# Attention sum, normaliser and output factor read from PSUM; the state's update as four column operations

## Chip, cores, metric

One core of a Trainium2 chip runs the whole program. The metric is the device time of one execution in microseconds (us). The engines are TensorE (PE, with its weight loads as PEld), VectorE (DVE), ScalarE (ACT), GpSimd (POOL) and SyncE (SP, which issues most transfers).

## The reference

Three layers follow each other: a gated linear attention (mLSTM), a mixture of experts with the best two of eight, and a gated feed-forward layer. The change is in the first. For 2 batches of 8 heads, 768 steps and head size 40 it computes:

```python
for t in range(S):
    m_new = np.maximum(f_gate[:, :, t] + m, i_gate[:, :, t])
    f_stab = np.exp(f_gate[:, :, t] + m - m_new)
    i_stab = np.exp(i_gate[:, :, t] - m_new)
    m = m_new
    C = f_stab[..., None, None] * C + i_stab[..., None, None] * np.einsum('bhd,bhe->bhde', vt, kt)
    n = f_stab[:, :, None] * n + i_stab[:, :, None] * kt
    h_tilde = np.einsum('bhde,bhe->bhd', C, qt)
    nq = np.einsum('bhd,bhd->bh', n, qt)[:, :, None]
    y[:, :, t] = 1.0 / (1.0 + np.exp(-o_gate[:, :, t])) * h_tilde / np.maximum(np.abs(nq), 1.0)
x = y.transpose(0, 2, 1, 3).reshape(B * S, H * D)
x = moe(x)          # top 2 of 8 experts, 320 -> 1024 -> 320
out = (silu(x @ w_gate) * (x @ w_val)) @ w_out   # 320 -> 1536 -> 320
```

## The kernel before

The 768 steps of a batch are cut into 6 chunks of 128 steps, so that there are 12 chunks `j`: 0 to 5 belong to the first batch, 6 to 11 to the second, and `c = j % 6` is the place within the batch. The recurrence is computed chunk by chunk. `scores` (L270) multiplies keys by queries, `weigh` (L278) multiplies the scores by decay weights that ACT and POOL have made (`prep_w`, L258), and `intra` (L307) multiplies the weights by the values, 41 columns a head (40 values and a column of ones, which gives the normaliser). Its result lies in columns 0 to 327 of a PSUM bank, `PY[j]`. `inter` (L290) multiplies the queries by the state of the earlier chunks, and `inter_y` (L299) scales that into an SBUF tile `t1`. `state` (L314) lets PE add this chunk's keys by values into columns 328 to 491 of the same bank, two heads above each other, so that four blocks `a` of 41 columns hold all eight; DVE multiplies the running state `Cs` by its decay (L328) and adds the bank's part (L329), and ACT copies `Cs` into `Cb` (L332), the operand of the next chunk's `inter`. In chunk 0 of a batch there is no earlier state, and `Cs` is copied (L326).

`norm` (L334) adds the two parts into an SBUF tile `y` (L338; a copy, L340, where c is 0), and makes the reciprocal of max(|n·q|, 1) in a small tile `dn` (L342 to L344). `x` holds the sigmoid of the output gate, and `emit_b` (L355) multiplies it by `y`, `emit_a` (L350) by `dn`. For chunk 0 `emit_a` runs on POOL. Then PE transposes `x` of that chunk (`gate_t`, L363, into a bank `pg`), and `gate_l` (L372) multiplies it by the router's weights.

The order on each engine is the order in which the code emits. Four strings of letters set it, one for the start and one each for the second, the middle and the last chunk; each letter calls one function with a chunk number. The one for the middle chunks is:

```python
BODY = 'GKzcWSdiwddctpqdyacdsdnmdvclcdde'
```

Here S is `scores` of the next chunk, i `inter`, w `weigh` of the next chunk, t `gate_t` of the chunk before, y `inter_y`, a `intra`, s `state`, n `norm`, m `emit_b`, l `gate_l` of the chunk before and e `emit_a`. So on PE the transposition of chunk j-1 (t) stands ahead of `intra` of chunk j (a), and waits for the last DVE operation of chunk j-1 (e). The letters d and c let in steps of the router (`route`, L376) and of its scatter by POOL; p lets in a piece of the experts' weights, which ACT rounds (L541) and POOL, in this stage, subtracts from the original (L542).

`PY[j]`, `pg` and a few others take turns in two PSUM banks of a pool named `po`. After the attention the experts (L641, L678) and the feed-forward layer (L641, L860) run on PE almost without a gap.

Of the kernel before, what the change touches and what calls it, by code (L numbers as in the profile page):

```python
# [7 lines left out]
F32 = mybir.dt.float32  # L8
# [5 lines left out]
OP = mybir.AluOpType  # L14
AX = mybir.AxisListType

B, H, S, D = 2, 8, 768, 40
# [11 lines left out]
DA = D + 1  # L29
# [59 lines left out]
def kernel(ctx, tc, qk, kvh, og, gates, cst, wgn, noise, w1, w2, w13, w2o, out):  # L89
    nc = tc.nc  # L90
    v, s, g, pe, sy = nc.vector, nc.scalar, nc.gpsimd, nc.tensor, nc.sync
# [52 lines left out]
    xs = dr.tile([NR + 2 * N, DM], F32, name="xs")  # L144
# [12 lines left out]
    at = atts.enter_context(tc.tile_pool(name="at", bufs=2, side="right", reuse_waits="tile"))  # L157
    eg = at.tile([128, NC, 2, 16], F32, name="eg", bufs=1)
    bc = at.tile([128, NC, 16], F32, name="bc", bufs=1)
    dec = at.tile([128, 8, NC], F32, name="dec", bufs=1)  # L160
    QK, KV, GB, W8, KS, YT, PY, PS = {}, {}, {}, {}, {}, {}, {}, {}
# [89 lines left out]
    Cs = at.tile([128, 4, DA], F32, name="Cs", bufs=1)  # L251
# [62 lines left out]
    def state(j):  # L314
        b, c = divmod(j, NC)
        if c == NC - 1:
            return
        va = KV[j][:, :, D:D + DA]
        q = H * DA
        for h in range(H):  # L320
            o = (h % 2) * 64
            pe.matmul(PY[j][o:o + 64, q + (h // 2) * DA:q + (h // 2 + 1) * DA], KS[j][:, h, :], va[:, h, :],
                      start=True, stop=True)
        pk = PY[j][:, q:q + 4 * DA].rearrange("p (a d) -> p a d", d=DA)
        if c == 0:
            v.tensor_copy(Cs, pk)  # L326
        else:
            v.tensor_tensor(out=Cs, in0=Cs, in1=dec[:, b * 4:b * 4 + 4, c, None].to_broadcast([128, 4, DA]), op=OP.mult)  # L328
            v.tensor_tensor(out=Cs, in0=Cs, in1=pk, op=OP.add)  # L329
        cb = Cb[(c + 1) % 2]  # L330
        for o in (0, 64):
            s.activation(cb[o:o + 64, :, o // 64, :], Cs[o:o + 64], AF.Copy)  # L332

    def norm(j):  # L334
        y = at.tile([128, H, DA], F32, name="y")
        py = PY[j][:, 0:H * DA].rearrange("p (h d) -> p h d", d=DA)
        if j % NC:
            v.tensor_tensor(out=y, in0=py, in1=YT[j], op=OP.add)  # L338
        else:
            v.tensor_copy(y, py)  # L340
        dn = at.tile([128, H], F32, name="dn")
        v.tensor_scalar(dn, y[:, :, D], -1.0, 1.0, op0=OP.mult, op1=OP.max)  # L342
        v.tensor_tensor(out=dn, in0=dn, in1=y[:, :, D], op=OP.max)
        v.reciprocal(dn, dn)  # L344
        YN[j] = (y, dn)

    def emit_a(j):
        y, dn = YN[j]
        xs = x[:, j, 0:DM].rearrange("p (h d) -> p h d", d=D)
        (v if j else g).tensor_tensor(out=xs, in0=xs, in1=dn[:, :, None].to_broadcast([128, H, D]), op=OP.mult)  # L350

    def emit_b(j):
        y, dn = YN[j]
# [653 lines left out]
    def early_piece(j):  # L1007
# [7 lines left out]
        "W": (2, prep_w),  # L1015
        "S": (1, scores), "K": (1, scale_k), "w": (1, weigh),
        "i": (0, inter), "y": (0, inter_y), "a": (0, intra), "s": (0, state),
        "n": (0, norm), "e": (0, emit_a), "m": (0, emit_b),
        "t": (-1, gate_t), "l": (-1, gate_l),
        "z": (0, lambda j: clear(3 if j == 2 else 2)), "p": (0, early_piece), "d": (0, lambda j: drip(1)), "c": (0, lambda j: drip_s(1)),  # L1020
# [149 lines left out]
```

## Time and profile before

| | us |
|---|---|
| median of 3 runs | 558.68 |
| the runs | 554.36, 558.68, 561.88 |
| the profiled execution | 555.08 |
| its span, first to last instruction | 553.4 |
| PE busy | 529.3 (96%) |
| DVE busy | 373.8 (68%) |
| ACT busy | 275.5 (50%) |
| POOL busy | 145.2 (26%) |

The attention takes about the first 116 us of the span. Busy shares are averages over all stages: PE is nearly always busy behind the attention and less so within it, so what DVE and POOL do matters in the attention first. PE matmul ends are modelled, and a few records can be missing. Starts are in us from the span's start, and an instruction of the same engine can begin a little ahead of the recorded end of the one in front of it.

### The profile page before, as it was taken

The page shows a single profiled execution, that of the slowest core. Times are in us where ns is not written, and L with a number is a line of the kernel's source. Part 1 is how long each engine was busy: PE and PEld are TensorE (multiplying, and loading weights), DVE is VectorE, ACT ScalarE, POOL GpSimd, SP SyncE. Part 2 cuts the span into 40 slices and gives each one's busy share as a digit, 9 for nine tenths or more (in the row PEclk, how much of TensorE's full clock was granted, in tenths as well). Part 3 has the DMA queues.
Part 4 walks back from the last instruction along what each step waited for, and adds up shares of the span by engine and source line. Part 5 has one row for each costly group of instructions (what it writes and reads, how often), then busy time and mean ns, then how long its engine had stood idle before and what let it go on. Part 6 is the DMA issues. An engine that isn't in the chain of part 4 may idle for free. (4 is left out here: it accounts for less than half of the span.)

```text
span 553.4 us, 9232 instructions
## 1 busy us (share of the span) xinstructions
PE 529.3 (96%) x3333; PEld 478.8 (87%) x3335; DVE 373.8 (68%) x833; ACT 275.5 (50%) x593; POOL 145.2 (26%) x175
## 2 busy tenths in 40 slices
PE   8998779889999999999999999999999999999997
PEld 4687678879898999989999999888888888888886
DVE  5584977858688897989898867787643434443332
ACT  5464545235566776876877664554332223222221
POOL 4153675455004432232322235233000000000000
PEclk8798877969999999999999999999999999999999
DMA  8799965553758787988987686461001000010001
GB/s 247 214 332 356 304 236 161 168 196 113 295 171 320 259 281 255 330 296 277 317 292 254 214 280 227 160 233 49 0 1 49 0 1 0 2 47 1 1 0 47
DMA packets 36882, 96.63 MB, mean 175 GB/s; under 512 B 4848, under 2 KB 17936, under 8 KB 36832
## 3 DMA queue, kind: packets, MB, share of 16 engines
q1 hardware_dynamic: 32208, 83.55, 44.9%
q0 software_dynamic: 2304, 7.87, 4.3%
q10 hardware_dynamic: 2320, 4.58, 2.4%
q8 instruction: 27, 0.44, 0.3%
q14 instruction: 23, 0.19, 0.1%
HBM read 72.70 MB, written 23.28 MB: 173 GB/s over the span
## 5 line engine op out<-in xcount | busy, mean ns | idle before, releaser
L678 PE MATMUL py<-wV,h 128*128 128x320 f32 (+1 forms) x624 | 106.6, 312 | 1.2 <-ACT ysb L689 0.8
L678 PEld LDWEIGHTS py<-wV,h 128*128 128x128 f32 (+1 forms) x624 | 95.6, 185 | 2.7 <-ACT ysb L689 1.2
L641 PE MATMUL ph<-xh,wU 128*128 128x416 f32 (+1 forms) x320 | 91.5, 336 | 0.4 <-PEq L719 0.4
L581 POOL TENSOR_TENSOR cq<-cq,csg 128x512 f32<-128x512 f32 (+1 forms) x27 | 38.5, 1425 | 121.0 <-ACT cq L580 96.7
L839 DVE TENSOR_TENSOR sg<-pg,sg 128x512 f32<-128x512 f32 x36 | 24.9, 691 | 58.2 <-ACT sg L838 58.2
L860 PE MATMUL py<-wV,uh 128*128 128x320 f32 x288 | 63.8, 309 | 0.0
L641 PEld LDWEIGHTS ph<-xh,wU 128*128 128x128 f32 x320 | 59.6, 195 | 2.5 <-ACTq L719 0.7
L542 DVE TENSOR_TENSOR wU<-stg,wU 128x512 fp32r<-128x512 f32 x72 | 54.1, 776 | 6.7 <-ACT wU L541 6.2
L838 ACT ACTIVATE sg<-pg 128x512 f32<-128x512 f32 x36 | 21.5, 598 | 66.0 <-PE pg L641 61.2
L848 ACT ACTIVATE uh<-u 128x512 fp32r<-128x512 f32 x36 | 22.8, 633 | 62.0 <-DVE u L840 62.0
L641 PE MATMUL ph<-xl,wU 128*128 128x416 f32 (+1 forms) x160 | 52.3, 327 | 0.1
L860 PEld LDWEIGHTS py<-wV,uh 128*128 128x128 f32 x288 | 49.5, 188 | 3.0
L641 PE MATMUL pg<-x2h,wU 128*128 128x512 f32 x144 | 51.4, 397 | 0.0
L641 PE MATMUL pv<-x2h,wU 128*128 128x512 f32 x144 | 50.6, 392 | 0.0
L541 ACT ACTIVATE wU<-stg 128x512 fp32r<-128x512 f32 x78 | 46.4, 624 | 7.4 <-DVE yt L687 4.6
L650 ACT ACTIVATE h<-ph 128x416 fp32r<-128x416 f32 (+1 forms) x80 | 35.6, 445 | 19.5 <-PE ph L641 17.6
L860 PE MATMUL py<-wV,ul 128*128 128x320 f32 x144 | 44.4, 309 | 0.0
L542 DVE TENSOR_TENSOR wV<-stg,wV 128x640 fp32r<-128x640 f32 x42 | 37.6, 906 | 3.4 <-ACT wV L541 3.3
L641 PE MATMUL ph<-xr,wU 128*128 128x416 f32 (+1 forms) x160 | 39.3, 327 | 0.3 <-DVE wU L542 0.3
L849 DVE TENSOR_TENSOR ul<-u,uh 128x512 fp32r<-128x512 f32 x36 | 24.9, 690 | 19.9 <-ACT uh L848 19.9
L777 POOL DMA_INDIRECT gy<-yg,ig__89 x24 | 25.2, 1051 | 48.0 <-DVE wU L542 26.8
L840 DVE TENSOR_TENSOR u<-pv,sg 128x512 f32<-128x512 f32 x36 | 24.9, 691 | 17.1 <-PE pv L641 16.7
(175 smaller groups left out, 1065.6 us busy)
## 6 DMA issues: line engine op xcount, KB each, us to landing
stg<-in_w_dram SPq DMA_DIRECT2D x20, 768.0 KB
stg<-in_w_dram SPq DMA_DIRECT2D x20, 640.0 KB
cw<-in_w_dram SPq DMA_DIRECT2D x18, 512.0 KB
gbt<-gp SPq DMA_DIRECT2D x10, 512.0 KB
f<-cq SPq DMA_DIRECT2D x18, 256.0 KB
stg<-f SPq DMA_DIRECT2D x6, 768.0 KB
kvt<-in_kvh_dram SPq DMA_DIRECT2D x12, 324.0 KB
QK<-in_qk_dram SPq DMA_DIRECT2D x24, 160.0 KB
```

Of the source, the lines that this page charges most:

```text
L541: s.activation(hi[:, c], ST[u][:, c], AF.Copy)
L542: (g if lo_pool[0] else v).tensor_tensor(out=lo[:, c], in0=ST[u][:, c], in1=hi[:, c], op=OP.subtract)
L581: g.tensor_tensor(out=q, in0=q, in1=sg, op=OP.mult)
L641: pe.matmul(ps_ap, a, b, start=(i == 0), stop=(i == len(seq) - 1))
L650: s.activation(h[:, 0:C], p[:, 0:C], AF.Relu)
L678: pe.matmul(yp[0:nr, 0:DM], x_, w, start=st and i == 0, stop=sp and i == 2)
L777: g.indirect_dma_start(out=y, out_offset=None, in_=yg[0:NR0] if j < NC else yg, in_offset=bass.IndirectOffsetOnAxis(ap=ig_[:, j, k:k + 1], ...
L839: v.tensor_tensor(out=sg, in0=pg, in1=sg, op=OP.mult)
L840: v.tensor_tensor(out=u, in0=pv, in1=sg, op=OP.mult)
L848: s.activation(uh, u, AF.Copy)
L849: v.tensor_tensor(out=ul, in0=u, in1=uh, op=OP.subtract)
L860: pe.matmul(OP_[q][a][:, 0:DM], x_[:, t], w[:, c], start=(f == 0 and i == 0), stop=(f == 11 and i == 2))
```

## The change

`norm` writes the sum back into the bank `PY[j]` in place of an SBUF tile, and leaves out the copy where c is 0: `y` is then the bank itself. A new small SBUF tile `dm` takes the first step of the normaliser; the second and the reciprocal are written into columns 492 to 499 of the same bank. `emit_b` and `emit_a` so read one operand from SBUF (`x`) and one from PSUM. `emit_a` of chunk 0 goes from POOL to DVE, as those of the other chunks. The state's decay and sum become one operation for each block of 41 columns, with the decay as one value a partition.

```diff
         else:
-            v.tensor_tensor(out=Cs, in0=Cs, in1=dec[:, b * 4:b * 4 + 4, c, None].to_broadcast([128, 4, DA]), op=OP.mult)
-            v.tensor_tensor(out=Cs, in0=Cs, in1=pk, op=OP.add)
+            for a in range(4):
+                v.scalar_tensor_tensor(Cs[:, a], Cs[:, a], dec[:, b * 4 + a, c:c + 1], pk[:, a], op0=OP.mult, op1=OP.add)
...
     def norm(j):
-        y = at.tile([128, H, DA], F32, name="y")
-        py = PY[j][:, 0:H * DA].rearrange("p (h d) -> p h d", d=DA)
+        y = PY[j][:, 0:H * DA].rearrange("p (h d) -> p h d", d=DA)
         if j % NC:
-            v.tensor_tensor(out=y, in0=py, in1=YT[j], op=OP.add)
-        else:
-            v.tensor_copy(y, py)
-        dn = at.tile([128, H], F32, name="dn")
-        v.tensor_scalar(dn, y[:, :, D], -1.0, 1.0, op0=OP.mult, op1=OP.max)
-        v.tensor_tensor(out=dn, in0=dn, in1=y[:, :, D], op=OP.max)
+            v.tensor_tensor(out=y, in0=y, in1=YT[j], op=OP.add)
+        dm = at.tile([128, H], F32, name="dm")
+        dn = PY[j][:, (H + 4) * DA:(H + 4) * DA + H]
+        v.tensor_scalar(dm, y[:, :, D], -1.0, 1.0, op0=OP.mult, op1=OP.max)
+        v.tensor_tensor(out=dn, in0=dm, in1=y[:, :, D], op=OP.max)
         v.reciprocal(dn, dn)
         YN[j] = (y, dn)
 
     def emit_a(j):
...
-        (v if j else g).tensor_tensor(out=xs, in0=xs, in1=dn[:, :, None].to_broadcast([128, H, D]), op=OP.mult)
+        v.tensor_tensor(out=xs, in0=xs, in1=dn[:, :, None].to_broadcast([128, H, D]), op=OP.mult)
```

On DVE, chunk 2 reads as follows before, from the scaling of the part of the earlier chunks to the weighing of the next scores (`t_526` is `t1`, `pg` the bank of the transposition, `W_487` the weights of chunk 4).

```order
L304 TENSOR_TENSOR t_526<-py,eg 128x328
L328 TENSOR_TENSOR Cs<-Cs,dec 128x164
L329 TENSOR_TENSOR Cs<-Cs,pY 128x164
L338 TENSOR_TENSOR y<-pY,t_526 128x328
L342 TENSOR_SCALAR dn<-y 128x8
L343 TENSOR_TENSOR dn<-dn,y 128x8
L344 RECIPROCAL dn<-dn 128x8
L355 TENSOR_TENSOR x<-x,y 128x320
L373 COPY lg<-pg 128x16
L350 TENSOR_TENSOR x<-x,dn 128x320
L281 TENSOR_TENSOR W_487<-pS,W_487 128x512 x2
```

The same chunk on DVE in the changed kernel, where the lines' numbers are those of the changed file:

```order
L304 TENSOR_TENSOR t_525<-py,eg 128x328
L329 SCALAR_TENSOR_TENSOR Cs<-Cs,dec,pY 128x41 x4
L337 TENSOR_TENSOR pY<-pY,t_525 128x328
L340 TENSOR_SCALAR dm<-pY 128x8
L341 TENSOR_TENSOR pY<-dm,pY 128x8
L342 RECIPROCAL pY<-pY 128x8
L353 TENSOR_TENSOR x<-x,pY 128x320
L371 COPY lg<-pg 128x16
L348 TENSOR_TENSOR x<-x,pY 128x320
L281 TENSOR_TENSOR W_486<-pS,W_486 128x512 x2
```

The decay no longer stands by itself ahead of the sum that needs PE's product; the rest keeps its place, with the bank in place of `y` and `dn`.

At the end of the start string, DVE before, from the first state (chunk 0) to the scaling in chunk 1:

```order
L326 COPY Cs<-pY 128x164
L340 COPY y<-pY 128x328
L342 TENSOR_SCALAR dn<-y 128x8
L343 TENSOR_TENSOR dn<-dn,y 128x8
L344 RECIPROCAL dn<-dn 128x8
L355 TENSOR_TENSOR x<-x,y 128x320
L1030 CAST slt<-ck 128x128
L281 TENSOR_TENSOR W_354<-pS,W_354 128x512 x2
```

And there now:

```order
L326 COPY Cs<-pY 128x164
L340 TENSOR_SCALAR dm<-pY 128x8
L341 TENSOR_TENSOR pY<-dm,pY 128x8
L342 RECIPROCAL pY<-pY 128x8
L353 TENSOR_TENSOR x<-x,pY 128x320
L348 TENSOR_TENSOR x<-x,pY 128x320
L1028 CAST slt<-ck 128x128
L281 TENSOR_TENSOR W_354<-pS,W_354 128x512 x2
```

The copy of 328 columns is gone, and `emit_a` of chunk 0 has come from POOL to stand behind `emit_b`. On PE, ACT and SP nothing changes its place.

## Rows read from the trace of the kernel before

**Rows 1.** Windows of 10 us: engines' busy us (instructions), PEclk, DMA share, GB/s.

```profile
40.00:50.00 10.00, 6.73 (x69) 5.75 (x67) 6.08 (x18) 4.27 (x14) 3.85 (x5) 1.00 1.04 373
...
80.00:90.00 10.00, 10.00 (x71) 9.14 (x71) 8.48 (x39) 4.14 (x12) 3.26 (x4) 0.55 0.57 189
```

**Rows 2.** The same view behind the attention (PE, PEld, DVE, ACT, POOL).

```profile
116.00:130.00 14.00, 13.91 (x80) 13.06 (x79) 7.15 (x43) 3.51 (x13) 5.90 (x11) 0.66 0.56 187
...
180.00:230.00 50.00, 50.00 (x303) 47.79 (x303) 43.88 (x86) 36.52 (x71) 17.29 (x15) 1.00 0.82 277
```

**Rows 3.** Waits of PE up to 116 us: total us, times, longest.

```profile
PE pg L363 <- DVE x L350: 9.4, 5, 4.5
```

**Rows 4.** Single lines: ns shortest/median/longest, first and last start.

```profile
L355 DVE TENSOR_TENSOR x<-x,y x12: 439/441/2096, 29.9 to 114.4; 128x320 f32<-128x320 f32 x12
...
L350 DVE TENSOR_TENSOR x<-x,dn x11: 478/492/841, 35.3 to 114.9; 128x320 f32<-128x320 f32 x11
...
L342 DVE TENSOR_SCALAR dn<-y x12: 170/171/1416, 28.9 to 112.2; 128x8 f32<-128x8 f32 x12
...
L338 DVE TENSOR_TENSOR y<-pY,t x10: 490/491/494, 33.8 to 111.6; 128x328 f32<-128x328 f32 x10
```

**Rows 5.** Timeline of DVE, chunks 6 and 7: start, us, operation [idle before].

```profile
74.84 0.33 DVE L326 COPY Cs<-pY 128x164 f32<-128x164 f32 x1 [3.79 <-PE pY L322]
75.09 0.49 DVE L340 COPY y<-pY 128x328 f32<-128x328 f32 x1
75.61 1.42 DVE L342 TENSOR_SCALAR dn<-y 128x8 f32<-128x8 f32 x1
77.06 1.22 DVE L343 TENSOR_TENSOR dn<-dn,y 128x8 f32<-128x8 f32 x1
...
78.91 0.80 DVE L350 TENSOR_TENSOR x<-x,dn 128x320 f32<-128x320 f32 x1
79.63 1.27 DVE L281 TENSOR_TENSOR W<-pS,W 128x512 f32<-128x512 f32 x2
80.83 0.17 DVE L397 TENSOR_TENSOR Lg<-ex,nz 128x24 f32<-128x24 f32 x1
81.03 0.18 DVE L398 TENSOR_TENSOR Lg<-Lg,lg 128x24 f32<-128x24 f32 x1
...
83.97 0.32 DVE L329 TENSOR_TENSOR Cs<-Cs,pY 128x164 f32<-128x164 f32 x1 [0.83 <-PE pY L322]
...
86.41 0.17 DVE L443 TENSOR_TENSOR pol<-pr,ck 128x24 f32<-128x24 f32 x1
```

**Rows 6.** Timeline of POOL around the same place and one chunk pair later.

```profile
78.50 0.87 POOL L267 TENSOR_SCALAR_AFFINE_SELECT W<-W 128x512 f32<-128x512 f32 x1 [0.25 <-ACT W L265]
...
101.15 1.29 POOL L542 TENSOR_TENSOR wU<-stg,wU 128x512 fp32r<-128x512 f32 x1
```

**Rows 7.** Timeline of PE, chunk 7.

```profile
79.86 0.52 PE L363 MATMUL pg<-ck,x 128*128 128x128 f32 x3 [2.07 <-DVE x L350]
```

**Rows 8.** Timeline of DVE, chunks 9 and 10.

```profile
99.40 0.32 DVE L329 TENSOR_TENSOR Cs<-Cs,pY 128x164 f32<-128x164 f32 x1 [1.18 <-PE pY L322]
99.64 0.49 DVE L338 TENSOR_TENSOR y<-pY,t 128x328 f32<-128x328 f32 x1
...
100.58 0.20 DVE L344 RECIPROCAL dn<-dn 128x8 f32<-128x8 f32 x1
100.70 2.10 DVE L355 TENSOR_TENSOR x<-x,y 128x320 f32<-128x320 f32 x1
...
106.82 0.32 DVE L328 TENSOR_TENSOR Cs<-Cs,dec 128x164 f32<-128x164 f32 x1
107.24 0.32 DVE L329 TENSOR_TENSOR Cs<-Cs,pY 128x164 f32<-128x164 f32 x1
107.48 0.18 DVE L417 TENSOR_TENSOR sel<-oh 128x24 f32<-128x24 f32 x1
```

**Rows 9.** Timeline of DVE in the experts: a small three-operand operation and its successor.

```profile
200.93 0.18 DVE L653 SCALAR_TENSOR_TENSOR h<-ph,h 128x32 fp32r<-128x32 f32 x1
201.03 0.58 DVE L627 TENSOR_TENSOR xl<-pxt,xh 128x416 fp32r<-128x416 f32 x1
```

## The prediction

> **What bounds the kernel now.** I read the busy time by stages first. Behind the attention PE has no gap: 50.00 of 50 us between 180 and 230 [rows 2]. So whatever moves the end of the attention, at about 116 us, moves the end of the program by as much. Within the attention no engine is full, and I ask which waits follow each other. The list of waits gives PE's largest one: 9.4 us in five waits, the transposition of a chunk waiting for `emit_a` of that chunk [rows 3]. PE is in order, so `intra` and `state` of the next chunk stand behind that wait; and DVE in turn waits for `state` before it can go on (0.83 and 1.18 us in two chunks) [rows 5, 8]. The path is a loop: DVE from the state's sum through norm and `emit_a`, PE from the transposition to `state`, DVE again.
>
> That holds from about 58 us on, chunks 4 to 11. Ahead of that the transfers are full (a share of 1.04 between 40 and 50 us, with PE busy for only 6.73 of 10) [rows 1]; what DVE saves or loses in chunks 0 to 3, the copy of chunk 0 and its `emit_a` from POOL among it, I count at nothing, with the key, query and gate loads as the cover. If that cover were gone, these chunks would pay or gain what the others do, a few tenths each.
>
> The last view is the one line by line. `emit_b` takes 441 ns in the median and once 2096; `emit_a` 492 and up to 841; the first step of the normaliser 171 and up to 1416 [rows 4]. All three work from SBUF alone. The sum, which has a PSUM operand, stays within 490 and 494 in all ten chunks [rows 4]. The stretched `emit_b`, at 100.70, runs beside a subtraction of weights on POOL from 101.15 that takes 1.29 us [rows 6, 8]. I read this as DVE and POOL keeping each other from SBUF, where the DVE operation needs nothing but SBUF operands. After the change none of these lines is such an operation.
>
> **The change part by part.** The terms are for the loop from 58 us on.
>
> 1. *Stalls of chunk 6.* The copy of 328 columns goes: its successor starts 0.52 us after it [rows 5]. The two first steps of the normaliser took 1.42 and 1.22 there against 0.17, so 1.25 and 1.05 us of stall go, and 0.31 of `emit_a`'s 0.80 against 0.49 [rows 4, 5]. That is 3.1 us on DVE. Not all of it is worth something. PE waited 2.07 us for this `emit_a` [rows 7], and that wait goes whole. But the next DVE work, the weighing, needs POOL's mask of the second half, which runs from 78.50 to 79.37 and depends on ACT, not on DVE [rows 6]. Its second half then takes some 0.6 us (half of 1.27 [rows 5]), so DVE reaches the router's first step at 80.0 and not at 80.83: 0.8 us. Further on it waited 0.83 us for PE [rows 5], and PE has 2.07 to give, so this wait goes too. Together 1.6 us, of 3.1. What is late next is POOL's mask. Bounds: 0.5 (the copy alone, if the stalls come back at the next SBUF operation) and 3.1.
>
> 2. *Stall of chunk 9.* 2.10 us of `emit_b` become 0.44: 1.66 us [rows 4, 8]. DVE's chain from there to the end of chunk 10 has no idle time, so I take 1.6. Bounds: 0 and 1.7.
>
> 3. *`emit_b` behind the reciprocal.* The normaliser lies in the bank that `emit_b` reads, and `emit_b` now waits for the reciprocal. Before, it started 0.12 us after it, ahead of that one's end at 0.20 [rows 8]; now at 0.20 or a little more, so +0.09. Its own time goes from 441 ns towards the sum's 491 for 8 columns more (8 ns) [rows 4]: +0.04. Eight chunks by 0.13: +1.0 us. Bounds: +0.6 and +1.6.
>
> 4. *Other operations in PSUM.* The sum and the reciprocal are written to PSUM, and the small steps read it. A small operation that reads PSUM took 0.17 us where one from SBUF took 0.18, both of 24 columns [rows 5]; so reading costs nothing here. No row shows DVE writing to PSUM. Near end: nothing. Far end: the fixed part of a small operation, 0.17 us, once more for each of the six operations that now touch PSUM, 1.0 us a chunk and 8 us over eight. I take nothing, since the nearest rows are those that read PSUM.
>
> [...]
>
> 5. *The state.* Before, the decay ran while DVE waited for PE, and only the sum came behind PE; the next operation started 0.24 us after it [rows 8]. Now all four come behind PE. A small three-operand operation of 32 columns holds DVE for 0.10 us until the next starts [rows 9]; 41 columns add 9 ns, so four take 0.44: +0.2 us in the chunks in which DVE waits for PE here, which are 7, 8 and 9. Where it does not (4 and 10) the decay and the sum together held it for 0.66 us (106.82 to 107.48 [rows 8]), now 0.44: -0.2. Sum: +0.2 us. Bounds: -0.3, and +1.6 if each took its whole 0.18 [rows 9]. ACT's copies of the state come 0.2 us later; PE needs them only behind the next scores, which run in the meantime.
>
> 6. *The bank* is now held to `emit_a`. No new wait comes of it: on PE the transposition of that chunk already waits for the same `emit_a`, and stands ahead of the next `intra` that takes the bank. The queues of SP and ACT keep their order; POOL loses one operation of chunk 0.
>
> Sum: -1.6 - 1.6 + 1.0 + 0 + 0.2 = -2.0 us. Against the profiled execution, 555.08, that is 553.1. That execution was among the faster: with the three runs (554.36, 558.68, 561.88) the four have a mean of 557.5, and the median of the three is 558.68. I place the change on the mean of four: 555.5.
>
> **The rivals.**
>
> *The stalls are handed on.* DVE and POOL still share SBUF; the router's steps are SBUF operations, and one free of a stall arrives earlier at the next POOL operation. For it: the gain of 3.1 us in chunk 6 brings DVE into the router's steps just when POOL has its next subtraction. Against it: the operations that were hit and matter most are those that leave SBUF. Terms 1 and 2 shrink to the copy's 0.5: -0.5 + 1.0 + 0.2 = +0.7, 558.2.
>
> [...]
>
> *PSUM is slow for DVE.* This is the one that ends on the other side, and its place is term 4: the six operations of a chunk that write or read the bank, all on the loop. They use up the whole gain at 0.25 us a chunk, some 40 ns each; from there on the kernel is slower. At half the far end, 4 us, the time is 559.5, at the far end 563.5. For it: writing from DVE is shown by no row. Against it: reading is, and costs nothing. [...]
>
> **How the numbers follow.** The forecast, 555.5, gets 0.45; the stalls handed on 0.2; the clock 0.15; slow PSUM 0.2. The range runs from 549.5 to 561.5: at the low end it takes in nearly all of the clock's gain, at the high end the far end of slow PSUM; the forecast's own, by its bounds, is 553.5 to 558.5. The runs of one kernel lie 7.5 us apart here, and a change of 2%, 11.2 us, is about what a measurement can tell from none. None of the cases' own times reaches it; the clock's 549.2 and slow PSUM's 563.5 come nearest, with the runs' spread. So 0.04 for faster, 0.93 for within 2%, 0.03 for slower.
>
> **What would show it.** Terms 1 and 2: `emit_b`, `emit_a` and the normaliser's steps have no instance above 0.6 us, and the transposition's wait of 9.4 us falls to about 6. If the router's small steps (ahead of the masks) have stretched instances in their place, the stalls were handed on. Term 3: `emit_b` starts 0.2 us behind the reciprocal. Term 4: the sum stays at 0.49 and the small steps at 0.17 to 0.20; 0.25 or more would mean slow PSUM. Term 5: four operations in about 0.44 us; 0.7 would cost another microsecond. Wrong as a whole it would be if the end of the attention did not move, or if PE had new gaps behind it.

## The result, and the profile after

| | before | after | ratio, 95% interval |
|---|---|---|---|
| median of four runs each, us | 559.54 (554.36 to 561.88) | 551.27 (546.73 to 555.02) | 0.9875, 0.9831 to 0.9919 |
| the same kernel once more, beside 23 runs of before | 555.18 | 547.22 (544.13 to 549.09) | 0.9834, 0.9782 to 0.9886 |

The changed kernel is faster by some 1.2 to 1.7%, 7 to 9 us. The forecast was 2.0 us less, 555.5 us: the direction held, and 551.27 lies in the range that was given (549.5 to 561.5), but the size did not hold. The repeat's 547.22 lies below that range, beside a before that was 4.4 us lower as well. The ratios leave out slower runs, of which the first profile of the changed kernel is one (granted clock 0.50 between 10 and 40 us, 0.89 in the second profile), so they differ from the quotients of the medians. The rows of "after" below are those of the second profile (e1), span 543.3 us.

The windows of after (busy us of PE, PEld, DVE, ACT, POOL with their instructions; granted clock, DMA share, GB/s), against [rows 1, 2]:

```profile
40.00:50.00 10.00, 9.05 (x79) 8.13 (x79) 5.44 (x17) 4.02 (x12) 3.26 (x4) 0.83 1.04 368
80.00:90.00 10.00, 8.50 (x66) 8.15 (x66) 6.98 (x34) 4.22 (x13) 4.53 (x6) 0.66 0.45 148
...
116.00:130.00 14.00, 13.77 (x113) 13.56 (x113) 11.80 (x51) 7.64 (x22) 9.77 (x18) 1.00 0.58 198
180.00:230.00 50.00, 50.00 (x303) 48.08 (x302) 45.14 (x87) 39.26 (x75) 15.05 (x13) 1.00 0.88 300
```

The row to look at is the third: behind the attention the granted clock is 1.00 where it was 0.66, and PE gets 113 matmul groups done in 14 us where it got 80 [rows 2]. The attention of this profile ended some 5 us earlier; shifted by as much, from 110 to 124 us, the window has 102 groups, at 1.00 as well. The transfers between 40 and 50 are as full as before (1.04), and the long stretch behind has as little gap as before.

PE's waits within the attention of after (total us, times, longest), against the 9.4 us of [rows 3]:

```profile
PE pr L421 <- DVE selb L416: 5.2, 3, 3.6
PE pg L361 <- DVE x L348: 2.8, 4, 1.4
```

The prediction's sign was a fall of the transposition's wait to about 6. It came: 5.4 us in e2, 5.6 in e7, 6.3 in the first profile of after. The largest of the five waits of [rows 3], 4.48 us behind the `emit_a` of chunk 5, is still there, 4.1 to 4.5 us, in every profile but this one and e10. Here it is 1.39, but PE waits 3.58 us for the router (L421) one chunk later.

The lines of after that answer to [rows 4] (ns shortest/median/longest, first and last start):

```profile
L353 DVE TENSOR_TENSOR x<-x,pY x12: 482/486/489, 27.2 to 109.6; 128x320 f32<-128x320 f32 x12
...
L348 DVE TENSOR_TENSOR x<-x,pY x12: 476/486/490, 27.7 to 110.1; 128x320 f32<-128x320 f32 x12
...
L342 DVE RECIPROCAL pY<-pY x12: 216/216/217, 26.9 to 109.0; 128x8 f32<-128x8 f32 x12
...
L340 DVE TENSOR_SCALAR dm<-pY x12: 144/166/168, 26.5 to 108.6; 128x8 f32<-128x8 f32 x12
...
L337 DVE TENSOR_TENSOR pY<-pY,t x10: 498/501/508, 32.5 to 108.1; 128x328 f32<-128x328 f32 x10
...
L329 DVE SCALAR_TENSOR_TENSOR Cs<-Cs,dec,pY x32: 244/251/260, 31.7 to 103.6; 128x41 f32<-128x41 f32 x32
```

No instance of `emit_b` (L353), `emit_a` (L348) or the normaliser is stretched any more: the longest lie within 7 ns of the median. The four operations of the state (L329) are dearer than forecast, 251 ns each.

The timeline of DVE in chunks 6 and 9 of after, against [rows 5, 8] (start, us, operation, idle before):

```profile
71.27 0.33 DVE L326 COPY Cs<-pY 128x164 f32<-128x164 f32 x1 [1.82 <-PE pY L322]
71.51 0.16 DVE L340 TENSOR_SCALAR dm<-pY 128x8 f32<-128x8 f32 x1
...
72.68 0.49 DVE L348 TENSOR_TENSOR x<-x,pY 128x320 f32<-128x320 f32 x1
73.09 1.28 DVE L281 TENSOR_TENSOR W<-pS,W 128x512 f32<-128x512 f32 x2
75.30 3.05 DVE L395 TENSOR_TENSOR Lg<-ex,nz 128x24 f32<-128x24 f32 x1 [0.93 <-ACT ex L392]
...
96.56 0.76 DVE L329 SCALAR_TENSOR_TENSOR Cs<-Cs,dec,pY 128x41 f32<-128x41 f32 x4 [1.49 <-PE pY L322]
97.36 0.51 DVE L337 TENSOR_TENSOR pY<-pY,t 128x328 f32<-128x328 f32 x1
...
98.31 0.22 DVE L342 RECIPROCAL pY<-pY 128x8 f32<-128x8 f32 x1
98.56 0.49 DVE L353 TENSOR_TENSOR x<-x,pY 128x320 f32<-128x320 f32 x1
```

From the state's copy to the start of `emit_a` it is 1.41 us now, 4.07 before. The weighing (L281) follows at once. Then the router's first step, whose operands both lie in SBUF, is held for 3.05 us beside POOL: one stall was handed on in this execution. The last rows are chunk 9, for terms 3 and 5.

**A place that the prediction did not look at** is chunk 11, the last. The timeline of before there, all engines:

```profile
112.94 1.54 POOL L542 TENSOR_TENSOR wV<-stg,wV 128x640 fp32r<-128x640 f32 x1 [6.18 <-ACT wV L541]
113.07 1.44 DVE L440 CAST cry<-cs 128x8 bf16<-128x8 f32 x1
113.21 0.59 PEld L624 LDWEIGHTS pxt<-ck,xgt 128*128 128x128 f32 x6
...
114.42 0.48 DVE L355 TENSOR_TENSOR x<-x,y 128x320 f32<-128x320 f32 x1
114.93 0.49 DVE L350 TENSOR_TENSOR x<-x,dn 128x320 f32<-128x320 f32 x1
...
115.57 0.87 PE L363 MATMUL pg<-ck,x 128*128 128x128 f32 x3 [1.56 <-DVE x L350]
...
116.10 0.54 PE L641 MATMUL ph<-xh,wU 128*128 128x224 f32 x1
```

A cast of 8 columns, the router's carry, begins 0.13 us behind a weight subtraction of POOL and lasts until that one ends (113.07 + 1.44 = 114.51; 112.94 + 1.54 = 114.48). `emit_b` and `emit_a` are late by it, and PE waits 1.56 us just ahead of the experts. What follows shows in windows of 2 us of before:

```profile
112.00:114.00 2.00, 1.85 (x12) 1.41 (x12) 1.83 (x7) 1.56 (x7) 1.06 (x1) 1.00 0.00 0
114.00:116.00 2.00, 0.44 (x3) 0.46 (x3) 1.89 (x7) 0.51 (x3) 1.70 (x3) 0.80 0.00 0
116.00:118.00 2.00, 1.91 (x10) 1.64 (x9) 1.32 (x5) 0.49 (x1) 1.72 (x3) 0.50 0.85 224
118.00:120.00 2.00, 2.00 (x9) 1.64 (x8) 0.39 (x1) 0.36 (x1) 1.57 (x5) 0.50 0.96 333
...
122.00:124.00 2.00, 2.00 (x11) 2.00 (x11) 0.39 (x1) 0.48 (x2) 0.23 (x2) 0.50 0.93 371
124.00:126.00 2.00, 2.00 (x12) 2.00 (x12) 1.62 (x14) 0.57 (x3) 0.00 (x0) 0.64 0.18 71
126.00:128.00 2.00, 2.00 (x21) 1.88 (x20) 1.52 (x9) 0.45 (x2) 0.00 (x0) 1.00 0.00 0
```

PE is busy for 0.44 of 2 us, and the granted clock, 1.00 until then, is 0.50 from 116 until about 125; PE is full all that time and does 9 to 12 groups in 2 us where it then does 21. The same place in after:

```profile
109.52 0.17 DVE L438 CAST cry<-cs 128x8 bf16<-128x8 f32 x1
109.53 1.57 POOL L540 TENSOR_TENSOR wV<-stg,wV 128x640 fp32r<-128x640 f32 x1 [6.54 <-ACT wV L539]
109.60 0.48 DVE L353 TENSOR_TENSOR x<-x,pY 128x320 f32<-128x320 f32 x1
...
110.12 0.49 DVE L348 TENSOR_TENSOR x<-x,pY 128x320 f32<-128x320 f32 x1
...
110.75 0.52 PE L361 MATMUL pg<-ck,x 128*128 128x128 f32 x3
...
111.02 0.35 PE L639 MATMUL ph<-xh,wU 128*128 128x224 f32 x1
```

Here the cast comes 0.01 us ahead of POOL and takes 0.17, and `emit_b` and `emit_a`, each with an operand in PSUM, run through beside POOL's whole 1.57 us. PE does not wait for the transposition, and its matmuls go on at 0.35 us where before took 0.54. A wait of 0.80 us that PE has at 112.17 leaves the clock at 1.00.

### The profile page after: what moved, and what is told of

Read it like the earlier page. It is cut to its first block, busy times and chain, and to the rows that moved or that the text cites. A ratio compares the mean times of both kernels' runs of the same rounds, so it can differ in the third digit from the quotient of the medians.

```text
span 553.3 us, 9234 instructions
## 1 busy us (share of the span) xinstructions
PE 532.3 (96%) x3333; PEld 479.3 (87%) x3335; DVE 370.1 (67%) x848; ACT 275.7 (50%) x593; POOL 142.9 (26%) x174
## 5 line engine op out<-in xcount | busy, mean ns | idle before, releaser
L639 PE MATMUL ph<-xh,wU 128*128 128x416 f32 (+1 forms) x320 | 89.5, 331 | 0.4 <-PEq L717 0.4
L639 PEld LDWEIGHTS ph<-xh,wU 128*128 128x128 f32 x320 | 57.9, 189 | 2.4 <-ACTq L717 0.7
L775 POOL DMA_INDIRECT gy<-yg,ig__89 x24 | 26.9, 1120 | 46.2 <-DVE wU L540 17.1
```

Source lines behind the costliest of these rows:

```text
L639: pe.matmul(ps_ap, a, b, start=(i == 0), stop=(i == len(seq) - 1))
L775: g.indirect_dma_start(out=y, out_offset=None, in_=yg[0:NR0] if j < NC else yg, in_offset=bass.IndirectOffsetOnAxis(ap=ig_[:, j, k:k + 1], ...
```

## Experiments

The theory to be tested: the gain comes from chunk 6 (term 1 of the prediction), from chunk 11, and from the clock behind it; the other chunks give nothing. The rivals: it comes a little from each chunk, or from the state's operations. Two numbers are read from each profile: the time from one chunk's `emit_a` to the next one's, and the time from the last `emit_a` to the end of the span. In before these are 9.5 us (chunk 5 to 6), 5.5 us (10 to 11) and 438.4 us.

**e1. The changed kernel again.** No edit.

> The changed kernel once more, beside its parts on the same chip. Both theories: a ratio to the kernel before of 0.983 to 0.992, about 5 to 9 us less. It gives the size that the parts have to add up to.

547.22 us, ratio 0.9834 (0.9782 to 0.9886). The three numbers: 4.9, 4.2 and 433.2 us. Its rows stand above.

**e2. The normaliser alone.** The changed kernel, with the state's two operations of before:

```diff
-            for a in range(4):
-                v.scalar_tensor_tensor(Cs[:, a], Cs[:, a], dec[:, b * 4 + a, c:c + 1], pk[:, a], op0=OP.mult, op1=OP.add)
+            v.tensor_tensor(out=Cs, in0=Cs, in1=dec[:, b * 4:b * 4 + 4, c, None].to_broadcast([128, 4, DA]), op=OP.mult)
+            v.tensor_tensor(out=Cs, in0=Cs, in1=pk, op=OP.add)
```

> Norm, emit_a and emit_b as in the changed kernel, the state's decay and sum as two operations as before. Theory A (the gain is the DVE operations that no longer need a second SBUF operand beside POOL, and the four state operations cost time, 0.67 us behind PE's product where the sum alone held DVE 0.24): faster than the changed kernel by another 1 to 2 us, ratio to before 0.980 to 0.988. Rival B (a good part of the gain is that the decay has left DVE's chain): slower than the changed kernel by 1 to 3 us, ratio 0.990 to 0.994. Rival C (the clock of the start, chance): nothing that stands out from the changed kernel either way, both within 0.3% of before.

548.28 us, 0.9837 (0.9783 to 0.9890); 6.7, 5.3 and 435.2 us. All of the gain is there without the state's part, but the 1 to 2 us more that theory A forecast are not. What the state's form does change is that the decay as an operation by itself has two SBUF operands. In chunk 8 of e2 and e7 it is held like the others, here in e7:

```profile
88.63 2.00 DVE L328 TENSOR_TENSOR Cs<-Cs,dec 128x164 f32<-128x164 f32 x1
```

The four operations, which read PSUM, were not held: 243 to 260 ns each in both profiles of after, 251 and 250 in the mean in e3 and e8. No gain in time shows from it.

**e3. The state alone.** The same edit the other way round, in the kernel before.

> The kernel before with the state's decay and sum as four operations, and nothing else. Theory A: slower by 1 to 2 us, ratio 1.002 to 1.004. Rival B: faster by 1 to 3 us, ratio 0.995 to 0.998. Rival C: no difference.

556.88 us, 1.0030 (0.9992 to 1.0068). The state's part alone gives nothing; what it costs lies between -0.1 and 0.7%, so theory A's 0.2 to 0.4% and no difference at all are both possible, and rival B falls. Chunks 6 and 11 have their stalls as before (9.3, 5.5, and 438.4 us behind).

**e4. Chunks 0 and 6 alone.** The kernel before, with sum and normaliser in PSUM only in the first chunk of each batch, and `emit_a` of chunk 0 on DVE:

```diff
         else:
...
+            y = py
+            dm = at.tile([128, H], F32, name="dm")
+            dn = PY[j][:, (H + 4) * DA:(H + 4) * DA + H]
...
-        (v if j else g).tensor_tensor(out=xs, in0=xs, in1=dn[:, :, None].to_broadcast([128, H, D]), op=OP.mult)
+        v.tensor_tensor(out=xs, in0=xs, in1=dn[:, :, None].to_broadcast([128, H, D]), op=OP.mult)
```

> The kernel before, with norm in PSUM only for the chunks without earlier state (0 and 6): the copy of 328 columns is left out there, the normaliser lies in the bank, and emit_a of chunk 0 is on DVE. Theory A: the stalls of chunk 6 (2.6 us) and its copy (0.5) go, so 2 to 4 us faster, ratio 0.993 to 0.997, some half of the whole change. A rival by which the gain is spread evenly over the chunks: 0.5 to 1.5 us, ratio 0.997 to 0.999.

552.15 us, 0.9963 (0.9932 to 0.9994). Chunk 5 to 6 takes 6.6 us, 2.9 less than before; chunk 11 has its stall (5.5 us, PE's wait 1.55), and 437.6 us follow.

**e5. Chunk 11 alone.** The kernel before, with sum and normaliser in PSUM only in the last chunk, and the carry's cast there on ACT, so that it does not stand ahead of `emit_b`:

```diff
+        if j == NJ - 1:
+            y = py
+            dm = at.tile([128, H], F32, name="dm")
+            dn = PY[j][:, (H + 4) * DA:(H + 4) * DA + H]
...
+            elif t0 == 6:
+                s.activation(cry, cs, AF.Copy)
             else:
                 v.tensor_copy(cry, cs)
```

> The kernel before; only in the last chunk, norm stays in PSUM (so emit_b and emit_a need one SBUF operand), and the router's small carry cast of 8 columns that stands ahead of emit_b there goes from DVE to ACT, so that DVE cannot be held by POOL's subtraction at that place. Theory A2 (the kernel before loses 1.3 us there, PE then idles 1.55 us just ahead of the experts, and its clock is low for the first 9 us of them): the cast's 1.4 us and PE's wait of 1.55 go, the granted clock of the 20 us from there on is 0.9 or more where the kernel before has 0.74, and the time falls by 3 to 5 us, ratio 0.991 to 0.995. Rival D (the clock behind the attention has nothing to do with that wait): the clock stays near 0.74, 1.0 to 1.5 us, ratio 0.997 to 0.998.

551.37 us, 0.9909 (0.9868 to 0.9949). Chunk 5 to 6 stays at 9.3; 10 to 11 takes 4.0, PE does not wait, the clock of the 20 us that follow is 1.00 (0.74 in before), and 434.5 us follow instead of 438.4. Rival D falls, and this one place is worth more than chunk 6. One operation with two SBUF operands is still in front of `emit_b`, the sum of the carry (8 columns); it begins at 115.21, 0.02 us ahead of POOL's subtraction, and takes 0.17.

**e6. Both.** e4's chunks and e5's together, the other nine as in before:

```diff
+        if j in (0, 6, 11):
+            y = py
```

> The kernel before with norm in PSUM for chunks 0, 6 and 11 only, and the carry cast of the last chunk on ACT. If the gain is the two places (chunk 6 and the last chunk with the clock behind it), their sum: 2 to 3 us of the run with chunks 0 and 6 alone plus 3 to 5, so 5 to 8 us, ratio 0.986 to 0.991, nearly the whole change. If the other chunks carry much of it: 3 to 4 us, ratio 0.993 to 0.995.

547.60 us, 0.9879 (0.9829 to 0.9929); 6.7, 4.0 and 433.4 us. The parts add up (-0.4% and -0.9% against -1.2%), and three chunks of twelve with the cast on ACT give what the whole change gave. "A little from each chunk" is not the main source; with intervals of 0.5% to either side, a us or two from the other nine is not excluded.

**e7. All chunks, and the cast on ACT.** e2 with the cast of e5.

> The changed kernel with the state's decay and sum as two operations as before, and the carry cast of the last chunk on ACT, so that DVE slips past POOL's subtraction there for certain and not by a hundredth of a us. Theory A2: as fast as the changed kernel or 1 to 2 us faster (ratio 0.979 to 0.985), with less spread between runs. Rival: the same as the changed kernel, the state's form and the cast both of no account.

548.16 us, 0.9900 (0.9843 to 0.9957); 6.4, 4.0 and 433.9 us. The nine other chunks add nothing to e6 that can be seen. Theory A2's 0.979 to 0.985 did not come, nor a smaller spread (546.99 to 553.73).

**e8. The normaliser's result in SBUF.** The changed kernel, but `emit_a` has two SBUF operands again:

```diff
-        dm = at.tile([128, H], F32, name="dm")
-        dn = PY[j][:, (H + 4) * DA:(H + 4) * DA + H]
+        dm = dn = at.tile([128, H], F32, name="dn")
```

> The changed kernel, but the normaliser stays in an SBUF tile: emit_b still reads the sum from PSUM, emit_a has two SBUF operands again. If two SBUF operands beside POOL are what stretches: emit_a has instances up to 0.8 us again while emit_b has none above 0.5; the two small normaliser steps stay unstretched except the reciprocal, which was never stretched. Time: 0 to 2 us slower than the changed kernel, ratio to before 0.984 to 0.988. If PSUM operands by themselves were the gain, and not the company of POOL: no stretched emit_a, and the same time.

551.22 us, 0.9936 (0.9905 to 0.9966): half of the gain is left, less than expected (0.984 to 0.988). `emit_a`, with two SBUF operands, takes up to 1.72 us and 761 ns in the mean over the twelve, 485 in e1. `emit_b`, with the sum in PSUM, has no instance above 0.48 us. So it is the second SBUF operand beside POOL that stretches. In chunk 11 this kernel fell into the trap of before, by 0.02 us:

```profile
110.02 1.54 POOL L539 TENSOR_TENSOR wV<-stg,wV 128x640 fp32r<-128x640 f32 x1 [6.28 <-ACT wV L538]
110.04 1.54 DVE L437 CAST cry<-cs 128x8 bf16<-128x8 f32 x1
...
112.64 0.87 PE L360 MATMUL pg<-ck,x 128*128 128x128 f32 x3 [1.54 <-DVE x L347]
```

The wait of PE is back with it, the clock of the next 20 us is 0.74, and 438.9 us follow. Chunk 6 keeps its gain (6.4 us to the start of its `emit_a`, and no longer than in before from there to chunk 10, though `emit_a` itself takes 1.61 there).

**e9. The cast alone.** The kernel before with e5's cast on ACT and nothing in PSUM.

> The kernel before, with one edit: the cast of the last route's carry (8 columns) on ACT instead of DVE. Theory (what leaves SBUF is what helps in chunk 11): emit_b, which still has two SBUF operands, comes next on DVE behind POOL's subtraction of 1.54 us and takes the stall over; emit_b 1.4 to 1.8 us in chunk 11, PE's wait for the transposition there stays at 1.3 to 1.6 us, the granted clock between 110 and 130 us stays at 0.7 to 0.8, last emit_a to the end 438 us; ratio 1.000 (0.997 to 1.003). Rival (the cast alone was the cause, whatever comes behind it): no stall in chunk 11, the wait gone, clock 1.00, last emit_a to the end 434.4 us; ratio 0.991 to 0.995.

556.57 us against 557.98 of before in these runs; ratio 0.9948 (0.9906 to 0.9990), below what the theory gave and within what the rival gave, with an interval that touches both. The profiled execution, at 557.19 us, went as the theory said:

```profile
114.14 1.54 POOL L544 TENSOR_TENSOR wV<-stg,wV 128x640 fp32r<-128x640 f32 x1 [6.18 <-ACT wV L543]
114.16 1.86 DVE L355 TENSOR_TENSOR x<-x,y 128x320 f32<-128x320 f32 x1
...
116.70 0.52 PE L363 MATMUL pg<-ck,x 128*128 128x128 f32 x3 [1.47 <-DVE x L350]
```

`emit_b` with two SBUF operands takes the stall over (1.86 us), PE waits 1.47, the clock from 112 to 132 is 0.83, and 439.4 us follow. So, in this execution, taking one operation out of POOL's way was not enough; the next one had to be out of it too. Whether every run of e9 went this way is not shown; one of them took 549.42 us.

**e10. A stall that the change left.** In e7 the router's `d` (L464) of the first three chunks is still held for 2.42 us (65.45 to 67.87). POOL runs a scatter (65.06 to 66.23) and then the subtraction issued in chunk 5 (66.30 to 67.84). Here DVE does that subtraction:

```diff
-LV = ()
+LV = (5,)
```

> e7 (normaliser in PSUM in all chunks, state in two operations, the carry's cast on ACT) with one edit: the weight piece issued in chunk 5 is subtracted on DVE instead of POOL. Theory (the router's step of 2.43 us in chunk 5 is a stall by POOL's subtraction, and PE's wait of about 4.5 us there follows from it): that step falls to about 0.3 us, DVE pays about 0.9 us for the subtraction, PE's wait falls by 1 to 2 us, start of chunk 5's to chunk 6's emit_a 0.5 to 1.3 us earlier; ratio to the kernel before 0.982 to 0.988, against 0.990 for e7. Rival (that step waits for something other than POOL, or DVE's own work eats it): PE's wait unchanged, ratio 0.988 to 0.993.

550.98 us, 0.9876 (0.9819 to 0.9932). The step falls to 0.34 us, PE's wait from 4.52 to 2.90, and chunk 4 to 5 takes 7.0 us instead of 8.6, but chunk 5 to 6 takes 7.9 instead of 6.4, so nothing is won. The timeline of DVE and the window of e10 show the new bound:

```profile
74.59 0.33 DVE L326 COPY Cs<-pY 128x164 f32<-128x164 f32 x1 [4.66 <-PE pY L322]
```

```profile
70.00:80.00 10.00, 10.00 (x65) 9.40 (x65) 4.45 (x21) 4.44 (x14) 7.46 (x11) 0.50 0.70 244
```

PE is full for all of these 10 us at a granted clock of 0.50, with 65 groups (0.83 and 84 in e7), and DVE waits 4.66 us for it. The theory had the stall and the wait right and their worth wrong: the ratio lies within its 0.982 to 0.988, but the gain was given back one chunk later.

**e11. The changed kernel with the cast on ACT.** The cast of e5, so that the 0.01 us does not decide.

> The changed kernel with one edit: the cast of the last route's carry on ACT. Theory (in the changed kernel this cast is ahead of POOL's subtraction by 0.01 to 0.2 us, so sometimes it may be caught): no stall in chunk 11 in the profile, PE without a wait of over 0.6 us there, last emit_a to the end 433 to 436 us, the ratio equal to that of the changed kernel or up to 0.3% better: 0.980 to 0.987. Rival (ACT's cast delays ACT's copy of the router's input or the weight piece by as much): same as e7, 0.990.

549.64 us, 0.9876 (0.9819 to 0.9933), between the two expectations. PE has no wait for the transposition of chunk 11, clock 1.00, 436.1 us behind. It is no better than the changed kernel.

**e12. POOL's subtraction later.** The kernel before; in the last chunk's order the weight piece (`p`) is issued behind `emit_a`:

```diff
-LAST = 'iyddatdnpdmcdeslccdd'
+LAST = 'iyddatdndmcdepslccdd'
```

> The kernel before, with one edit: in the order of the last chunk the weight piece is issued behind emit_a instead of ahead of emit_b, so that ACT's cast of it, and with it POOL's subtraction, come later; DVE's and PE's orders are unchanged. Theory (the POOL subtraction of 1.54 us that begins 0.13 us ahead of the 8-column cast is what stretches that cast to 1.44 us): the cast takes 0.15 to 0.25 us; POOL's subtraction then begins 0.5 us or more later, so either emit_a or emit_b is caught instead (1.0 to 1.7 us, the wait of PE stays, ratio 1.000) or, if POOL's scatter comes first and holds it up past emit_a, nothing is, PE's wait is gone, the clock behind it at 1.00 and the ratio 0.990 to 0.995. Rival (the cast is slow for a reason of its own, such as its place behind cs): it stays at 1.44 us wherever POOL's subtraction begins.

557.10 us, 1.0007 (0.9973 to 1.0041). It came out as neither branch had it: one scatter of POOL went ahead of the subtraction, so this began 1.42 us behind the sum of chunk 11 instead of 1.29, not half a microsecond later, and caught the cast again:

```profile
114.56 1.54 POOL L542 TENSOR_TENSOR wV<-stg,wV 128x640 fp32r<-128x640 f32 x1
114.57 1.57 DVE L440 CAST cry<-cs 128x8 bf16<-128x8 f32 x1
...
117.21 0.52 PE L363 MATMUL pg<-ck,x 128*128 128x128 f32 x3 [1.70 <-DVE x L350]
```

As a way to free the cast it failed. As a measurement it gives one more pair: 0.01 us behind POOL's start costs as much as 0.13. The rival that the cast is slow for a reason of its own does not stand beside the 0.17 us of after.

## Why the prediction was right in direction and short in size

**Term 1, chunk 6: mis-sized, -1.6 for what measured -2.8.** The stalls went as described. The step that failed is "the next DVE work, the weighing, needs POOL's mask of the second half, which runs from 78.50 to 79.37". The mask of [rows 6] belongs to the weights of the chunk after: the order on POOL and DVE gives one mask pair to each weighing, and the pair of the weighing at 79.63 [rows 5] had run at 73.00. In e1 the next pair comes behind the weighing of 73.09, which so cannot need it (first line before, the others e1):

```profile
73.00 1.22 POOL L267 TENSOR_SCALAR_AFFINE_SELECT W<-W 128x512 f32<-128x512 f32 x2
...
71.22 1.22 POOL L267 TENSOR_SCALAR_AFFINE_SELECT W<-W 128x512 f32<-128x512 f32 x2
...
75.85 1.21 POOL L267 TENSOR_SCALAR_AFFINE_SELECT W<-W 128x512 f32<-128x512 f32 x2
```

So DVE was held by nothing, and the time from the `emit_a` of chunk 5 to that of chunk 6 fell from 9.3 to 9.5 us (before, e3, e5, e9, e12) to 6.3 to 6.9 (after, e2, e4, e6, e7, e8, e11; 4.9 in e1). The upper bound, 3.1, was nearly reached. PE's wait of 2.07 us there went whole, as forecast, but PE then waits for a step of the router (L421): 0.5 to 1.3 us in after, e2, e4, e6, e7, e8 and e11, 3.58 in e1.

**Terms 2, 3 and 5 in chunks 7 to 10: about nothing in sum.** From the `emit_a` of chunk 6 to that of chunk 10 it takes 30.0 to 30.9 us where their normaliser is as before (seven profiles, mean 30.6), and 29.1 to 33.2 where the sum is in PSUM in all (seven profiles, mean 30.6). The forecast gave these chunks about -0.9 (-1.6, four times 0.13, and 0.2), which the spread does not exclude. Term 2 by itself: the stall of chunk 9 went as described, and its worth was mis-sized. It is there in all eight profiles in which an edited operation of that chunk has SBUF operands alone, though not always on `emit_b`: 2.10 to 2.12 us there in before, e4 and e6, 1.72 to 1.83 on `emit_a` in e3 and e8, 1.61 to 1.75 on the first step of the normaliser in e5, e9 and e12. In the other six none of these lines is stretched. From the `emit_a` of chunk 8 to that of chunk 10 it takes 13.6 to 14.1 us with the stall (mean 13.8) and 12.4 to 14.3 without (mean 13.3), some 0.5 us for the 1.6 forecast. What is saved can be handed on: in e1 the router's step of 3.05 us, just behind chunk 6, had PE wait 3.6 us, and these chunks took 33.2 us.

Term 3: `emit_b` starts 0.25 us behind the reciprocal's start (98.31 to 98.56), 0.12 before [rows 8], and takes 486 ns instead of 441: +0.17 a chunk, forecast +0.13. e8 shows which part of the change this is: with the sum in PSUM but the normaliser in SBUF, `emit_b` starts 0.12 us behind the reciprocal again (92.08 to 92.20 in chunk 8) and takes 432 to 437 ns in eleven of its twelve chunks. The price is that of the normaliser lying in the bank, not of reading PSUM.

Term 4: nothing, as forecast. The steps that read PSUM take 166 to 170 ns, where [rows 4] has 171. Writing to PSUM costs 10 ns in the sum (501 against 491) and 13 in the reciprocal, which reads it as well (216 against 203). The rival "PSUM is slow for DVE" falls.

Term 5: mis-sized. The four operations hold DVE for 0.67 us (103.05 to 103.72) to 0.80 (96.56 to 97.36), forecast 0.44. The row it was read from has a number as its scalar [rows 9]; here the scalar is a column, and one takes 251 ns, not 180 + 9. The nearer row of before is L789, with a column as its scalar: 546 ns in the median for 320 columns, where `emit_a` of that width takes 492 [rows 4]. The prediction did not use it. What it costs the kernel is not settled: e3 has +0.3%, 1.7 us, where the bound given was +1.6, with an interval of -0.4 to +3.8 us. The prediction did not see that the decay was itself an SBUF-only operation that POOL could hold (2.00 us in e2 and e7).

Term 6 and the first chunks: no new wait on the bank. From chunk 1 to chunk 4 it takes 25.5 us before and 25.0 in e1, and 24.7 to 26.2 in all profiles but the first of after (22.0): no gain that can be told from the spread, as forecast.

**What was not in the sum: chunk 11 and the clock.** "What bounds" lists the stretched lines among those that the change edits. The carry's cast is not edited, so its 1.44 us were not looked for; PE's 1.56 us behind it was one of the five waits of [rows 3] and was not followed to its cause. In after `emit_b` and `emit_a` are out of POOL's way, and the cast comes ahead of POOL: from chunk 10 to 11 it takes 4.0 to 4.2 us instead of 5.5 in e1, e5, e6, e7, e10 and e11 (5.3 in after's first profile and in e2, where DVE waits for PE instead). Behind it, from the last `emit_a` to the end, it took 437.6 to 439.4 us in the six profiles in which PE had waited there (before, e3, e4, e8, e9, e12; mean 438.5; clock of the 20 us from there 0.74 to 0.83) and 433.2 to 438.3 in the eight in which it had not (mean 435.1; clock 1.00 in all eight): -3.4. The eight are of two kinds: 433.2 to 435.2 in e1, e2, e5, e6 and e7, and 436.1 to 438.3 in after's first profile, e10 and e11, in which PE waits once more, 0.9 to 1.0 us, at a step of the router (L421) some 10 us later. What brings that wait was not tried.

So -2.8, about 0, -0.2 to -1.4 and -3.4 make -6.4 to -7.6 us, and 7 to 9 were measured; a us or two stays open. That the result lay in the range was in part luck: its low end came from the clock's 549.2, and the sum that gave the forecast held nothing of this stretch. No run shows the term behind that 549.2; the runs show 3.4 us behind chunk 11, at a granted clock of 1.00 in place of 0.74 to 0.83. PE's wait of 2.07 us in chunk 6 does not decide it: in e4 that one is gone, the one in chunk 11 is there, and the clock behind is still 0.83. The rival of stalls handed on was real as a mechanism (e1, e9) and wrong as a total.

The rule behind the stalls was read from rows and held: none of the chunk's operations with an operand in PSUM was stretched in after, in 12 chunks each (in e1 none above 508 ns, the longest of the sum). The pairs above add that the start decides in chunk 11: 0.17 us when the cast is 0.01 us ahead of the subtraction, 1.44 to 1.57 when it is 0.01 to 0.13 behind. By the prediction's own reading the cast at 113.07, which works from SBUF alone, belonged on the list.

Being ahead of the subtraction is not enough, though. The stretched `emit_b` of [rows 8] began at 100.70, 0.45 us ahead of the subtraction of [rows 6], and still ended only 0.36 us behind it. POOL was then in a scatter that led straight into the subtraction:

```profile
100.11 0.99 POOL L476 DMA_INDIRECT xs<-x,is__88  x1 [0.17 <-issue]
```

The router's step of e7 is a second such case (65.45, in the scatter of 65.06 to 66.23), and without the subtraction behind the scatter it took 0.34 us (e10). A sum of 8 columns in e12 began beside a scatter too, at 114.37, and took its 0.17. So when a scatter holds DVE is not settled here.

## What to carry to other kernels

When operands are moved to PSUM to get out of POOL's way, list every SBUF-only operation between the last PE wait and the next, edited or not: the first one behind a POOL operation can take the whole of it (a cast of 8 columns took 1.57 us beside a subtraction of 1.54 in e12). Follow each wait of PE to the end of its stage, and look at the granted clock behind it: here waits of 1.5 to 1.7 us just ahead of a full stretch went with 3.4 us more behind them in the mean, about twice themselves. Edit first the places that are on the path; here three chunks of twelve, with one cast moved to ACT, gave as much as all twelve. And leave no gain to a race: in the changed kernel the cast came 0.01 us ahead of POOL in one profile.

## What was not expected of the hardware

- A DVE operation of 8 columns can last 1.57 us: it ends with POOL's subtraction, 0.03 or 0.04 us behind it (before and e12). In e1 one of 24 columns, begun at 75.30, was held until 78.35, with POOL busy almost without a gap from 75.16 to 78.28 in three lines.
- Some hundredths of a us decide whether the cast is held: 0.17 us at 0.01 ahead of POOL's subtraction (e1), 1.57 at 0.01 behind (e12). The changed kernel had it ahead by 0.01 and 0.22 us in two profiles, e8 behind by 0.02.
- PE was idle for 1.56 us ahead of the experts, and the granted clock was 0.50 for some 9 us after that with PE full. Without that wait it was 1.00 over the 20 us from the last `emit_a` in all eight profiles.
- A three-operand DVE operation of 41 columns takes 251 ns with a column as its scalar; the one with a number took 180 ns for 32 columns [rows 9].
